# Polysketch attention with a phase mixer: wide numerator products, matrix-half sums on VectorE, a balance by ScalarE and a new order behind the first part

## The chip, the cores and the metric

One core of one Trainium2 chip runs the whole program. TensorE multiplies matrices into PSUM (eight banks of 512 32-bit words in each of 128 partitions), VectorE, ScalarE and GpSimd compute elementwise, and SyncE (SP), ScalarE and GpSimd issue DMAs. The metric is the device time of one execution in microseconds (us); lower is better. Where this text says "the profile", it means one execution taken by the hardware profiler, with a page of tables and a trace of single instructions behind it.

## The reference

The shapes are B = 4 batches, H = 4 heads, S = 1088 positions, D = 32 numbers a head, r = 8. An attention with the product features phi(x) = (S1 x) outer (S2 x), 64 numbers, gives x of 1088 x 128 for each batch; a phase mixer follows:

```python
def phi(x):
    a = np.einsum('rd,bhsd->bhsr', S1, x)
    b = np.einsum('rd,bhsd->bhsr', S2, x)
    return np.einsum('bhsi,bhsj->bhsij', a, b).reshape(*x.shape[:-1], r * r)
q_p, k_p = (phi(q), phi(k))
kv = np.einsum('bhsf,bhsd->bhfd', k_p, v)
z = np.sum(k_p, axis=2)
num = np.einsum('bhsf,bhfd->bhsd', q_p, kv)
den = np.einsum('bhsf,bhf->bhs', q_p, z)[..., None] + 1e-06
x = (num / den)                        # then (B,H,S,D) -> (B,S,H*D)
theta = x @ w_theta
zr, zi = x * np.cos(theta), x * np.sin(theta)
y = np.einsum('ts,bsd->btd', w_tok_r, zr) + np.einsum('ts,bsd->btd', w_tok_i, zi)
u = x + y
out = u + np.maximum(u @ w_ch, 0.0)
```

The weights (S1, S2, and the four of the mixer) come as 64-bit floating-point words.

## The kernel before

**How it is written.** No loop of the program runs on the chip in the order of its source. Each piece of work is an `Op` (an engine, a function that emits a few instructions, the buffers that it writes and reads), numbered as it is created by `Layout.op` (L203). A table of numbers, `ORDER` (L34), says in which order all 1020 operations are emitted, and each engine then runs its own ones strictly in that order. An operation that must wait holds up everything behind it on the same engine. A second table, `STARTS` (L80), gives each operation a planned start. `run` (L248) uses it to give buffers their places: memory is divided into classes of equal slots (L344: "big" 22 of 1152 words a partition, "zs" 5 of 2176, "hf" 6 of 576, "g3" 5 of 768, "g1" 6 of 384, "sm" 13 of 192, "ps" the eight PSUM banks and so on). `issue` (L267) uses it to put small matmuls without use (`spin`, L427, into a bank that nobody reads) into planned gaps of TensorE during the first part, from operation `first` (39 spins) to operation `last`.

**Stages.** (1) The 64-bit weights are unpacked into 32-bit ones on the chip: for each of 17 rows of the token matrix w_tok (128 x 1088, loaded by SP), two ScalarE passes (L643, L645) and two VectorE steps. (2) From k and v come the sums `kv` and the row sums for the denominators, batch by batch (batches 2 and 3 together). (3) From q come the levels, products of q with the sketch in several exact slices (`levels`, L1034; its function `whole`, L1049, multiplies by a stationary block of 128 positions at a time, nine blocks, though the last one has 64 real positions only). (4) `outputs_x` (L1088) makes x. (5) theta, the cosines and sines and z = (x cos, x sin) follow. (6) The token mix multiplies z by the rows. Batches 0 and 1 do it directly (`mix_row`, L1256; 17 rows, three column pieces). Batches 2 and 3 are done together by `winograd` (L1352): seven half-size products in place of eight. (7) `finish` (L1282) multiplies by w_ch, adds, transposes and stores.

**outputs_x for batches 2 and 3** (`QUADS`). The nine chunks of 128 positions are worked in three groups of three. For each group VectorE forms the outer products `qp` (768 numbers a partition, L1101), transposes them in blocks of 32 x 32 into `qt` (L1109), and the operation `quads` (L1112) multiplies: 32 matrix products, each with a stationary 32 x 32 tile of the sums `bd` and 96 moving columns (3 chunks x 32 positions), into four PSUM banks `xq`. Four ScalarE copies (L1121) then bring the banks into `xT`. The three groups are three such rounds a batch, six in both; a product of 32-bit numbers leaves two matmul records in the trace.

**balance** (L1229). The two batches' x are scaled to like size before they are mixed: VectorE reduces each `xT` (1152 numbers a partition) to the maximum of magnitudes (L1232), five short steps keep only the exponents of the two maxima (`ratio`, L1235) and form powers of two. ScalarE scales x of batch 3 by one of them (`even`, column 4), and VectorE takes it out again at the end (`add`, column 5). Any number of about the right size would serve, since only its exponent is used and what is multiplied is divided again.

**turn** (`XTURN`, batches 1 to 3). x is needed in the other orientation too. VectorE transposes in 32 x 32 blocks (L1160), SP writes the result to DRAM (`far`, L1161) and reads it back in four DMAs in another arrangement (L1165).

**winograd** (L1352). The four quarters of the token matrix (rows by imaginary or real part and column half of 544) are combined by `asum` ("1" to "4", eight differences or sums of 128 x 544 each), z by `zsub`. The products "1", "2", "5", "6", "3", "7", "4" run in this order of creation, each in two column parts of 384 and 160 (`PARTS`), eight matmuls a part. `APOOL` (L153) names the sums that GpSimd makes:

```python
APOOL = ("4", "3")
...
E, e = (G, "G") if name in APOOL else (V, "V")          # in asum
```

After a product, `add` (VectorE) brings its bank into `xT`; `ends` multiplies the 64 last positions; `done` calls `finish` for each part.

**finish and the end.** `finish` multiplies by w_ch, adds max(u w_ch, 0) to u (VectorE), and `turn` (L1302) transposes and, for the first half of batch 3 (`ends`), issues the four stores in the same operation: one by ScalarE, one by SP, two by GpSimd. The last 160 columns of this half go through `finish_turned` (L1329) instead: two TensorE transpositions, a ScalarE copy into the free part of `xT` (L1338), two products, all in one operation, then a VectorE step and two stores.

Of the kernel before, what the change touches and what calls it, by code (L numbers as in the profile page):

```python
# [10 lines left out]
F32 = mybir.dt.float32  # L11
# [67 lines left out]
)  # L79
STARTS = (  # L80
# [58 lines left out]
)  # L139
WARM = 0  # L140
FILL = 5.0
LOAD_LEAD = 60.0
RAW_LEAD = 30.0
CHAINS = ((0,), (1,), (2, 3))
# [1399 lines left out]
```

## Time and profile before

| What | Value |
|---|---|
| runs | 217.95, 218.06, 217.34 us; median 217.95 |
| profiled execution, first start to last end (span) | 215.9 us |
| TensorE busy (PE) | 208.9 us, 97% of the span |
| TensorE weight loads (PEld) | 152.8 us, 71% |
| VectorE busy (DVE) | 174.3 us, 81% |
| ScalarE busy (ACT) | 114.5 us, 53% |
| GpSimd busy (POOL) | 59.7 us, 28% |
| sums of matrix halves on GpSimd, 128 x 544 | 16 of 1458 ns, 22.1 us |
| sums and differences on VectorE, 128 x 544 | 8 of 1204 ns (`asum` "2") and 8 of 715 ns (`asum` "1") |
| numerator products, 32x32 tiles with 96 columns | 384 records, 5.8 us busy in sum, mean 252 ns |
| their ScalarE copies, L1121 | 24 of 252 ns |
| largest magnitudes by VectorE, L1232 | 2 of 1344 ns |
| ScalarE pass that also sums, L991 | 1170 ns, and 199 ns to read the sum |

In the profile's rows, "L399" is the line of the kernel that emits the instruction; many have the line of a helper (L399 is `mm`, L379 `tt`, L386 `stt`). "ps<-big,zs" names the class of the output and of the inputs. "128*128" is the tile of TensorE that a matmul uses (rows x columns), then follow shape and type of the moving operand, and "x10" is the number of records. Records of TensorE are pipelined and overlap, so a mean duration is not the time that one takes from the engine; the distance of the starts is. A bracket such as "[2.70 <-PE ps L399]" says how long the engine stood idle ahead of the instruction, in us, and what ended that.

### The profile page before, as it was taken

To read this page: it belongs to the slowest core of one execution; us is meant where nothing else is said; L and a number is where in the kernel's file an instruction comes from. 1 tells how busy PE (TensorE), PEld (TensorE's weight loads), DVE (VectorE), ACT (ScalarE), POOL (GpSimd) and SP (SyncE) were. 2 spreads that over 40 slices of the span, in tenths; PEclk is the share of its full clock that TensorE was granted. 3 is DMA by queue.
4 is the path that set the end of the run, shared out by engine and by line. 5 is a ranking of instruction groups with operands and counts; after the bars stand their busy time and mean duration, and the time that the engine had idled before them with its cause. 6 is when DMAs were issued, how large, how long until landed. Compare 5 with 4: busy or idle time off the path is not lost.

```text
span 215.9 us, 5832 instructions
## 1 busy us (share of the span) xinstructions
PE 208.9 (97%) x2396; PEld 152.8 (71%) x2396; DVE 174.3 (81%) x343; ACT 114.5 (53%) x256; POOL 59.7 (28%) x105
## 2 busy tenths in 40 slices
PE   7899999999999999999999999999999999999992
PEld 7677798868866666866668666667677776666781
DVE  1799998999999998999999798885994747456263
ACT  4899989999998895798704233363810000000000
POOL 1272740306400000604004100000006489950403
PEclk9999999999999999999999999999999999999998
DMA  6999999995998993192002402424050420010735
GB/s 222 395 418 419 384 365 420 425 315 97 360 285 267 416 432 145 75 308 45 0 0 32 74 3 112 114 109 112 2 88 15 67 39 0 0 23 8 125 55 103
DMA packets 28046, 37.09 MB, mean 172 GB/s; under 512 B 20564, under 2 KB 23044, under 8 KB 25844
## 3 DMA queue, kind: packets, MB, share of 16 engines
q1 hardware_dynamic: 22868, 31.86, 42.4%
q0 software_dynamic: 1552, 3.25, 7.2%
q10 hardware_dynamic: 3600, 1.62, 2.8%
q8 instruction: 19, 0.31, 0.6%
q14 instruction: 7, 0.06, 0.1%
HBM read 29.84 MB, written 4.00 MB: 157 GB/s over the span
## 4 chain that ended last, share of the span: by engine, by line
PE 63%; DMA 18%; ACT 14%; issue 2%; SPq 1%; DVE 1%; POOL 1%; POOLq 0%; ACTq 0%
PE ps L399 61%; DMA zs<-w_tok 13%; DMA big<-k_l 5%; ACT big L645 4%; ACT big L643 3%; ACT lv L1056 1%; PE ps L1131 1%; ACT big L1021 1%; ACT g L1199 1%; ACT g L1202 1%; ACT g L1205 1%; ACT g L1203 1%; POOL out L1299 1%; SPq L671 0%; ACT g L1135 0%
## 5 line engine op out<-in xcount | busy, mean ns | idle before, releaser
L399 PE MATMUL ps<-big,zs 128*128 128x384 f32 (+2 forms) x380 | 110.5, 436 | 0.0
L399 PEld LDWEIGHTS ps<-big,zs 128*128 128x128 f32 x380 | 66.9, 190 | 32.5
L379 POOL TENSOR_TENSOR big<-big,big 128x544 f32<-128x544 f32 x16 | 22.1, 1458 | 48.6 <-DVE big L379 44.6
L399 PE MATMUL ps<-big,big 128*32 128x32 f32 (+2 forms) x352 | 22.8, 234 | 0.0
L643 ACT ACTIVATE big<-zs 128x1088 f32<-128x1088 f32 x17 | 20.9, 1231 | 1.5 <-DMA zs<-w_tok 0.9
L379 DVE CUSTOM_DVE_ANT_0 big<-big,big 128x2176 uint16<-128x2176 uint16 x17 | 21.5, 1275 | 0.0
L645 ACT ACTIVATE big<-zs 128x1088 int32<-128x1088 uint32 (+1 forms) x18 | 21.4, 1194 | 0.3 <-DMA zs<-w_tok 0.3
L1338 ACT COPY big<-ps 80x256 f32<-80x256 f32 x1 | 0.4, 368 | 39.6 <-DMA out<-g 39.6
L399 PEld LDWEIGHTS ps<-big,big 128*32 128x32 f32 (+1 forms) x352 | 15.3, 124 | 6.8 <-issue 0.8
L1276 ACT COPY g<-ps 128x384 f32<-128x384 f32 (+1 forms) x6 | 2.5, 466 | 23.4 <-PE ps L399 23.4
L379 DVE TENSOR_TENSOR big<-big 128x544 f32<-128x544 f32 x8 | 9.5, 1204 | 5.6 <-PE ps L399 5.6
L383 DVE TENSOR_SCALAR big<-big 128x1088 int32<-128x1088 int32 x17 | 12.2, 719 | 0.0
L379 POOL TENSOR_TENSOR mf<-mv,sm 128x32 f32<-128x32 f16 (+1 forms) x3 | 0.8, 262 | 39.1 <-DVE sm L379 39.1
L428 PE MATMUL ps<-idle 128*128 128x112 bf16 (+1 forms) x67 | 10.0, 312 | 1.3 <-POOL idle L430 1.3
L379 DVE TENSOR_TENSOR g<-lv 128x768 f32<-128x768 f32 x12 | 11.1, 950 | 0.1
L399 PEld LDWEIGHTS ps<-w,big 128*128 128x128 f32 (+1 forms) x76 | 9.8, 189 | 1.4
L379 DVE TENSOR_TENSOR big<-big,hf 128x1152 f32<-128x1152 f32 x8 | 10.7, 1351 | 0.0
L399 PE MATMUL ps<-w,big 128*128 128x128 f32 (+1 forms) x76 | 10.5, 278 | 0.0
L399 PE MATMUL ps<-sbk,g 128*128 128x64 f32 x72 | 10.0, 276 | 0.3 <-ACT g L793 0.3
L379 DVE TENSOR_TENSOR zs<-zs,g 128x384 f32<-128x384 f32 (+2 forms) x24 | 9.8, 447 | 0.2
L386 DVE SCALAR_TENSOR_TENSOR big<-ps,even,big 128x384 f32<-128x384 f32 (+1 forms) x10 | 4.8, 493 | 6.3 <-PE ps L399 6.2
L1199 ACT ACTIVATE g<-ps 128x384 f32<-128x384 f32 x12 | 5.9, 504 | 7.3 <-PE ps L399 7.3
(199 smaller groups left out, 379.2 us busy)
## 6 DMA issues: line engine op xcount, KB each, us to landing
zs<-w_tok SPq DMA_DIRECT2D x17, 1088.0 KB, 10.6
big<-k_l SPq DMA_DIRECT2D x5, 576.0 KB, 13.2
big<-v_l SPq DMA_DIRECT2D x4, 576.0 KB, 15.6
big<-q_l SPq DMA_DIRECT2D x3, 576.0 KB, 10.7
big<-hf POOLq DMA_DIRECT2D x3, 576.0 KB, 10.0
far<-zs SPq DMA_DIRECT2D x3, 576.0 KB, 2.8
zs<-far SPq DMA_DIRECT2D x12, 144.0 KB, 4.3
big<-k_l ACTq DMA_DIRECT2D x2, 576.0 KB, 4.4
```

The costliest lines, as they stand in the source:

```text
L379: eng.tensor_tensor(out=o, in0=a, in1=b, op=f)
L383: (eng or V).tensor_scalar(out=o, in0=a, scalar1=s1, scalar2=s2, op0=op0, **kw)
L386: (eng or V).scalar_tensor_tensor(out=o, in0=a, scalar=s, in1=b, op0=op0, op1=op1)
L399: T.matmul(o, lhs, rhs, start=start, stop=stop, skip_group_check=True)
L428: T.matmul(nowhere()[:, :n], idle()[:, 0:P], idle()[:, :n], start=True, stop=True, skip_group_check=True)
L643: op("A", 0.22 + n * 0.0009, lambda: A.activation(dfn(), words_of(raw(), n)[1].bitcast(F32), AF.Prelu, scale=2.0**-112, alpha=-(2.0**32)), ...
L645: op("A", 0.22 + n * 0.0009, lambda: A.activation(stp(), words_of(raw(), n)[0].bitcast(U32), AF.Copy, scale=2.0**-29), [stp], [raw])
L1021: op("A", act(GW) + 0.1, lambda g=g, tr=tr: A.activation(f()[:, g * GW:(g + 1) * GW], tr(), AF.Copy, scale=s()[:, 0:1]), [(f, g)], [tr, (s ...
L1056: op("A", act(480), lambda g=g, lp=lp: A.copy(lv().rearrange("p l (c n) -> p l c n", n=HR)[:, :, g * GC:(g + 1) * GC], lp().rearrange("p c ...
L1131: T.transpose(tr()[:, i * P:(i + 1) * P], qp()[:, i * H + 2 * n:i * H + 2 * n + 2].rearrange("p h i j -> p (h i j)"), ident())
L1199: op("A", act(GW), lambda cs=cs, th=th: A.activation(cs()[:, 0], th(), AF.Copy, bias=ROUND), [(cs, 0)], [th])
L1276: op("A", act(w), lambda: A.copy(u(), yp()[:, :w]), [uT], [yp])
```

## The change

1. **Numerator.** For batches 2 and 3, `qt` is one buffer of class "zs" for all nine chunks (2304 words, so the class grows from 2176). The three groups' outer products and transpositions are made as before; then one `quads` makes 32 products of 288 columns into four banks, followed by four copies of 288 columns.
2. **Sums of halves.** `APOOL` is empty: `asum` "3" and "4" go to VectorE like "1" and "2".
3. **Balance.** In place of VectorE's maximum, ScalarE passes over `xT` with the function Abs and an accumulator; the passes' output goes to a scratch buffer "dump" of class "hf". `ratio` is unchanged.
4. **finish_turned** is split into four operations (transpositions, ScalarE copy, products, VectorE step) and the two stores, and its result has a buffer `yb` of class "g1" of its own.
5. **whole** in `levels` uses, for the last chunk, a stationary block of the 64 real positions only.
6. **Order.** The first 265 operations of `ORDER` stay as they are but for operations 0 and 1 (the memset of `idle` and the 39 spins), which are now named first. All that follows is in another order. `STARTS` is gone: `GAPS` says after which operations of the first part a `spin` is emitted (27 in all, and the one at `last`, as before), and `SLOTS` gives each of 393 buffers its slot.
7. **Classes.** "hf" goes from 6 slots to 5 and "sm" from 13 to 12.

At the end of the new order TensorE has product 3's first part (384 columns) up to its last matmul, then the output product of batch 2's second half (its second part), the transpositions and the products of the turned piece, and last the output product of batch 3's first part, `out3_0_0`. VectorE ends with the two sums from PSUM, batch 2's last step and transposition, the turned piece's step, and then the step of `out3_0_0` and its `turn` with the four stores. In the order before, `out3_0_0` stood ahead of product 3's second part.

```diff
 ORDER = (
-    29, 32, 4, 2, 5, 0, 1, 3, 34, ...
+    0, 1, 29, 32, 4, 2, 5, 3, 34, ...
...
-STARTS = (
+GAPS = {11: 3, 57: 3, 79: 3, 110: 1, 203: 8, 153: 1, 77: 5, 86: 2, 163: 1}
+SLOTS = (
...
-APOOL = ("4", "3")
+APOOL = ()
...
     def run(self):
-        slots = {c: [[0.0, None] for _ in range(n)] for c, (n, _) in self.classes.items()}
...
         self.order = [self.ops[i] for i in ORDER]
-        for o, at in zip(self.order, STARTS):
...
+        for b, slot in zip([b for b in self.bufs if b.cls is not None], SLOTS):
+            b.slot = slot
...
         for o in self.order:
-            if o.eng == "P":
...
+            for _ in range(GAPS.get(o.i, 0)):
+                fill()
...
-        "zs": (5, 2176),
+        "zs": (5, 2304),
...
-        "hf": (6, 576),
+        "hf": (5, 576),
...
-        "sm": (13, 192),
+        "sm": (12, 192),
...
             def whole(g=g, o=o):
                 for i in range(GC):
-                    x = f()[:, (g * GC + i) * P:(g * GC + i + 1) * P]
-                    mm(o(i)[:, 2 * HR:], x, mf[b]().rearrange("p t h r -> p (t h r)"), False, i == GC - 1)
+                    c = g * GC + i
+                    n = min(P, S - c * P)
+                    x = f()[:, c * P:c * P + n]
+                    mm(o(i)[:n, 2 * HR:], x, mf[b]().rearrange("p t h r -> p (t h r)"), False, i == GC - 1)
...
+        qt = buf("zs", (NC, H, 2, SQ), F32, "qt") if b in QUADS else None
...
             if b in QUADS:
-                qt = buf("g3", (GC, H, 2, SQ), F32, "qt")
-                xq = [buf("ps", (GC, SQ), F32, "xq") for _ in range(NQ)]
...
+                vop(CH * R * R, lambda g=g, qp=qp: V.transpose(
+                    out=qt()[:, g * GC:(g + 1) * GC].rearrange("p c h f t -> p (c h f t)"),
+                    in_=qp().rearrange("p n i j -> p (n i j)")), [(qt, g)], [qp])
                 continue
...
+        if b in QUADS:
+            xq = [buf("ps", (NC, SQ), F32, "xq") for _ in range(NQ)]
+
+            def quads():
+                for f in range(2):
+                    for j in range(NQ):
+                        for h in range(H):
+                            u = slice(j * SQ, (j + 1) * SQ)
+                            mm(xq[j]()[h * D:(h + 1) * D], bd()[u, f, h], qt()[u, :, h, f], f == 0, f == 1)
+
+            op("P", QUAD, quads, xq, [bd, qt], hold=[xt])
+            for j in range(NQ):
+                op("A", act(NC * SQ), lambda j=j: A.copy(
+                    xt().rearrange("p (c j t) -> p c j t", j=NQ, t=SQ)[:, :, j], xq[j]()), ...)
...
-            vop(NC * P, lambda j=j, b=b: V.tensor_reduce(out=even()[:, j:j + 1], in_=xT[b](), axis=AX.X, op=ALU.max,
-                                                         apply_absolute_value=True), [(even, j)], [xT[b]])
+            dump = buf("hf", (NC * P,), BF16, "dump")
+            op("A", act(NC * P) + 0.1, lambda j=j, b=b, dump=dump: A.activation(
+                dump(), xT[b](), AF.Abs, accum_out=even()[:, j:j + 1]), [dump, (even, j)], [xT[b]])
...
     def finish_turned(b, t0, w, u, keys, due):
-        y = lambda: xT[b]()[:n, 0:2 * DM]
+        yb = buf("g1", (2 * DM,), F32, "yb")
+        y = lambda: yb()[:n]
...
+        op("P", 0.2, turned, [pu], keys, hold=[yb])
+        op("A", act(2 * DM), lambda: A.copy(y(), pu()[:n, 0:2 * DM]), [yb], [pu])
+        op("P", 0.35, products, [po], keys + [w2])
+        vop(2 * DM, lambda: stt(y(), po()[:n, 0:2 * DM], 0.0, y(), ALU.max, ALU.add), [yb], [po])
```

More of the change, by code (lines that the diff above doesn't have):

```diff
@@ L44 @@
     163, 164, 165, 166, 211, 39, 191, 167, 173, 448, 114, 168, 212, 175, 244, 449, 331, 176, 192, 177, 266, 450, 336,
[34 rows of a table removed]
-)
-STARTS = (
[58 rows of a table removed]
[33 rows of a table added]
+)
+GAPS = {11: 3, 57: 3, 79: 3, 110: 1, 203: 8, 153: 1, 77: 5, 86: 2, 163: 1}
+SLOTS = (
[11 rows of a table added]
 )
 WARM = 0
-FILL = 5.0
 LOAD_LEAD = 60.0
@@ L157 @@
 UDMA = (True, True, False, False)
-TILE16, TILE32, TILE64, QUAD = 0.045, 0.12, 0.15, 0.65
+TILE16, TILE32, TILE64, QUAD = 0.045, 0.12, 0.15, 1.25
 ADD_FLY = 9.0
@@ L248, in run, with issue @@
     def run(self):
-        slots = {c: [[0.0, None] for _ in range(n)] for c, (n, _) in self.classes.items()}
-        for b in self.bufs:
-            b.left = len(b.ops)
         self.order = [self.ops[i] for i in ORDER]
-        for o, at in zip(self.order, STARTS):
-            o.start = at / 100.0
-            o.end = o.start + o.dur + o.fly
-            for b in o.bufs:
-                if b.slot is None and b.cls is not None:
-                    free = [(s[0], i) for i, s in enumerate(slots[b.cls]) if s[1] is None]
-                    b.slot = min(free)[1]
-                    slots[b.cls][b.slot][1] = b
-            for b in o.bufs:
-                b.left -= 1
-                b.end = max(b.end, o.end)
-                if not b.left and b.slot is not None:
-                    slots[b.cls][b.slot] = [b.end, None]
-    def issue(self, pools, fill, span):
-        last, on = 0.0, False
-        for o in self.order:
-            if o.eng == "P":
-                if on:
-                    for _ in range(int((o.start - last - 0.08) * FILL)):
-                        fill()
-                last, on = o.end, on and o is not span[1] or o is span[0]
+        for b, slot in zip([b for b in self.bufs if b.cls is not None], SLOTS):
+            b.slot = slot
+    def issue(self, pools, fill):
+        for o in self.order:
+            for _ in range(GAPS.get(o.i, 0)):
+                fill()
             for b in o.bufs:
@@ L430 @@
     op("G", 0.3, lambda: G.memset(idle(), 0.0), [idle], [], due=-20.0)
-    first = op("P", 3.2, lambda: [spin(112) for _ in range(39)], [nowhere], [idle], due=-10.0)
+    op("P", 3.2, lambda: [spin(112) for _ in range(39)], [nowhere], [idle], due=-10.0)
     op("V", 1.25, constants, [hm, bdm, halfpi, ones], [])
@@ L1145, in outputs_x @@
                cells(xt, g * GW, (g + 1) * GW), [xp])
+        if b in QUADS:
+            at("num", b)
+            xq = [buf("ps", (NC, SQ), F32, "xq") for _ in range(NQ)]
[8 more added lines that the diff above has]
+                op("A", act(NC * SQ), lambda j=j: A.copy(
+                    xt().rearrange("p (c j t) -> p c j t", j=NQ, t=SQ)[:, :, j], xq[j]()), [(xt, ("q", j)) if j < NQ - 1 else xt], [xq[j]])
         src = xt
@@ L1331, in finish_turned, with turned @@
         n = w // 2
-        y = lambda: xT[b]()[:n, 0:2 * DM]
-        def products():
-            parts = [u()[:, c * n:(c + 1) * n] for c in range(2)]
-            for c, uc in enumerate(parts):
-                T.transpose(pu()[:n, c * DM:(c + 1) * DM], uc, ident())
-            A.copy(y(), pu()[:n, 0:2 * DM])
-            for c, uc in enumerate(parts):
-                mm(po()[:n, c * DM:(c + 1) * DM], uc, w2()[:, 1], True, True)
-        op("P", w * 4 / 2400 + 0.01, products, [po, pu], keys + [w2])
-        vop(w, lambda: stt(y(), po()[:n, 0:2 * DM], 0.0, y(), ALU.max, ALU.add), keys, [po])
-        vop(w, lambda: None, [], keys)
+        yb = buf("g1", (2 * DM,), F32, "yb")
+        y = lambda: yb()[:n]
+        def turned():
+            for c in range(2):
+                T.transpose(pu()[:n, c * DM:(c + 1) * DM], u()[:, c * n:(c + 1) * n], ident())
+        def products():
+            for c in range(2):
+                mm(po()[:n, c * DM:(c + 1) * DM], u()[:, c * n:(c + 1) * n], w2()[:, 1], True, True)
+        op("P", 0.2, turned, [pu], keys, hold=[yb])
+        op("A", act(2 * DM), lambda: A.copy(y(), pu()[:n, 0:2 * DM]), [yb], [pu])
+        op("P", 0.35, products, [po], keys + [w2])
+        vop(2 * DM, lambda: stt(y(), po()[:n, 0:2 * DM], 0.0, y(), ALU.max, ALU.add), [yb], [po])
         def store(E, c):
             E.dma_start(out[b, t0 + c * n:t0 + (c + 1) * n, :], y()[:, c * DM:(c + 1) * DM])
-        op("S", w * P * 2 / 100e3, lambda: store(SY, 0), [], keys, due, lk=2)
-        op("A", 0.92, lambda: store(A, 1), [], keys, due, fly=2.1)
+        op("S", w * P * 2 / 100e3, lambda: store(SY, 0), [], [yb], due, lk=2)
+        op("A", 0.92, lambda: store(A, 1), [], [yb], due, fly=2.1)
     def winograd(t):
@@ L1469 @@
         if not bs[0]:
-            last = op("P", 0.1, spin, [nowhere], [kvb[WARM]] if WARM < B else [idle])
+            op("P", 0.1, spin, [nowhere], [kvb[WARM]] if WARM < B else [idle])
     for b in range(B):
@@ L1499 @@
     with tc.manual_schedule():
-        L.issue(pools, spin, (first, last))
+        L.issue(pools, spin)
 def kernel(q, k, v, S1, S2, moe_w_theta, moe_w_tok_r, moe_w_tok_i, moe_w_ch):
```

13 lines of the change are left out of this document (removed), and 138 rows, old and new, of tables (ORDER, SLOTS, STARTS).

## The prediction

> **What bounds the kernel now.** I read the page first, then the TensorE rows by shape for 140 to 210 us, then the timeline of single engines.
>
> ```profile
> span 215.9 us, 5832 instructions
> PE 208.9 (97%) x2396; PEld 152.8 (71%) x2396; DVE 174.3 (81%) x343; ACT 114.5 (53%) x256; POOL 59.7 (28%) x105
> ...
> PE 63%; DMA 18%; ACT 14%; issue 2%; SPq 1%; DVE 1%; POOL 1%; POOLq 0%; ACTq 0%
> ```
>
> Busy PE is modelled, so 97% proves little by itself. Counting does: from 140 to 210 us the rows by shape hold 154 records of 384 columns, 120 of 160, 12 of 320 and 12 of 128. Starts in the timeline stand 0.325, 0.135, 0.27 and 0.11 us apart (136.99 to 137.64 for two of 384, 207.59 to 207.86, 149.92 to 150.46, 138.93 to 139.59 for six). 154 x 0.325 + 120 x 0.135 + 12 x 0.27 + 12 x 0.11 = 70.8 us in 70: TensorE is full. The same count comes out near the length of the window back to about 45 us, and the list of TensorE's waits after 45 us holds one of 0.2 us. So from 45 us on the time is TensorE's work, any wait that the new order opens, and what follows its last large product.
>
> ```profile
> 67.38 0.48 PE L399 MATMUL ps<-big,big 128*32 128x32 f32 x32
> ...
> 77.49 0.88 PE L399 MATMUL ps<-g,big 128*32 128x64 f32 x48
> ...
> 119.09 0.96 PE L399 MATMUL ps<-g,g 32*32 32x96 f32 x64
> 119.98 3.39 PE L399 MATMUL ps<-big,zs 128*128 128x384 f32 x10
> ```
>
> Second number: from first start to last end; the start of the next row tells what a block takes. One numerator block (32 products, 64 records: a 32-bit product leaves two) holds TensorE for 119.98 - 119.09 = 0.89 us, 13.9 ns a record. The rows after the first two start at 67.79 and 78.42: 12.8 ns a record at 32 columns, 19.4 at 64.
>
> ```profile
> 208.50 2.34 PE L399 MATMUL ps<-big,zs 128*128 128x160 f32 x16
> ...
> 210.30 0.57 DVE L1303 STREAM_TRANSPOSE g<-big 128x384 f32<-128x384 f32 x1
> ...
> 210.68 0.43 PE L399 MATMUL ps<-big,w 128*128 128x160 f32 x2
> 210.88 0.38 DVE L386 SCALAR_TENSOR_TENSOR big<-ps,even,big 128x160 f32<-128x160 f32 x1
> 211.17 1.81 POOL L1299 DMA_DIRECT2D out<-g  x3 [0.50 <-DVE g L1303]
> ```
>
> The end: the last large product hands over at T = 210.68; GpSimd's three store issues run from 211.17 to 212.98, so the last starts at 212.38 = T + 1.7 (the last of SP and ScalarE start at 212.79 and 212.73, T + 2.1); the span ends at T + 5.2.
>
> **Numerator products.** Six blocks of 96 columns become two of 288: the same 64 records each, three times as wide. No row shows 32x32 tiles at 288. Lower bound: width is free, 0.89 us a block. Upper: time goes with columns, 2.67. Nearest rows: with four tiles side by side, 32 more columns cost 19.4 - 12.8 = 6.6 ns, 0.206 ns a column; with sixteen tiles a quarter of that, 0.052. So 13.9 + 192 x 0.052 = 23.8 ns a record, 1.5 us a block; I take that. Sum: 6 x 0.89 = 5.34 becomes 3.0, **-2.3 us** (-3.6 to 0). The copies on ScalarE fall from 24 of 252 ns to 8 of about 0.41 us (384 columns take 0.49); from 120 to 160 us ScalarE is 24 to 62% busy, so that is worth nothing to the end. The block now waits for all three transposed groups and four free banks, and the rows of batch 1 stand behind it on TensorE, with their PSUM readers on ScalarE behind those. Before, the third group was ready at 134.4 for a block at 135.35, 0.9 us ahead; in the new order the last bank and the last group come about as far ahead, so 0 (at most 1 us for each of the two blocks if that cover is gone).
>
> **The end.** In the new order the last large record is the 384-wide one of product 3, then TensorE has out2_1_1, the two transpositions, the two products of the turned piece, and last the 384-wide output product out3_0_0, which before came at 207.86, ahead of 16 large records. So T comes 0.65 us earlier (one pair of 384). After T, by rows: VectorE takes the sum from PSUM to T + 0.8 (0.2 handover, 0.61), out2_1_1's two steps to 1.4, the turned piece to 1.8 (its copy on ScalarE is done by 1.05); TensorE needs 0.27 + 0.2 + 0.43 before out3_0_0 starts at 0.9, which ends at 1.55; VectorE's two steps of it run from 1.85 to 2.9. Only then are its four stores issued (they sit inside the transposing step `turn`), two of them by GpSimd at 0.62 us each: the last issue starts at T + 3.75 against T + 1.7. **+2.05 - 0.65 = +1.4 us** (0.2 to 2.05: if the stores of SP and ScalarE land last in both, it is T + 2.95 against T + 2.1, +0.85 - 0.65; at the other end T comes no earlier).
>
> **Sums of halves on VectorE.**
>
> ```profile
> 175.66 5.47 POOL L379 TENSOR_TENSOR big<-big,big 128x544 f32<-128x544 f32 x4
> ...
> 177.13 4.59 DVE L379 TENSOR_TENSOR big<-big 128x544 f32<-128x544 f32 x1 [2.70 <-PE ps L399]
> ```
>
> Sixteen sums leave GpSimd (1.458 us each, 22.1 busy) and join VectorE at 0.64 (two in 1.36 less the overlap): +10.3 us. VectorE idles some 26 us after 140, so they fit; had they no cover, each late one would cost 0.64 at the product that reads it. One difference on VectorE took 4.59 us where its neighbours take 0.72, while GpSimd's sums ran; that 3.9 us goes. The Trainium skill, SBUF — State Buffer, "Who interferes with whom", says that a VectorE operation with two SBUF inputs and a GpSimd one exclude each other for a whole instruction. By that every GpSimd sum would hold VectorE, up to 22 us; the trace shows one such hold, and other pairs of the two that overlapped unharmed (162.84 to 164.2), so the row decides: 3.9 us of a spare engine.
> I checked in the new order where these results are read. The tightest: product 7's third row needs its sum and the sum from PSUM of product 6; those come 2 to 4 us ahead. Product 4's first matmul follows the last of product 7 by 0.8 us, and needs the 0.6 us read of that bank plus 0.2: **+0.1 us**.
>
> **Balance on ScalarE.** Two VectorE reductions (1.344 us each) become two ScalarE passes with an accumulator; the row of the same form (line 991) is 1.17 plus 0.2. Path of batch 3 from the end of its numerator block: 0.2 + 4 copies 1.65 + 1.37 + the ratio 0.85 + two theta copies that ScalarE does first, 0.15 beyond the ratio + scaling 1.25 + transposition 1.4 + trip through DRAM 6.4 (142.26 to the end of its transfers at 148.7) + z and first difference 2.0 = 15.3 us. TensorE has queued between (counted: 6 + 6 large of 0.645, 12 of 0.272, seven rows of batch 1, three theta, one output product) 17.7 us. Cover 2.4 us, so 0.
>
> **Moves.** The first 265 operations keep their order on every engine; the spin and its memset, now written first, were first on their engines before. Fills stay 28. After that all queues are in another order; SP's changes most: the load of v2 goes behind batch 1's trip through DRAM and row 12. From the last numerator product of batch 1 TensorE has 15.7 us of work (counted in the new order) before the first product with v2. In that time: copy 0.7, transposition 1.4, first half of the trip 2.9, its four read issues 1.75, v2's issue 0.4, together 7.2 us; loads of this size land 4.4 us (k on ScalarE's queue) to 15.6 us (v on SP's, amid others) after issue, so v2 is 4.1 us early to 7.1 late. Between the ends: row 16 and the same trip, 2.3 MB like the new row 12, trip and v2, were moved between 90 and 98.5 us, which puts v2 some 5 us after its issue, 3.5 early. I take 0. The last chunk's `whole` product loads 64 columns where it loaded 128: 8 loads less by half of 0.11, at most -0.4; **-0.1**, since the stream then limits. The turned piece in a tile of its own, smaller pools and fixed slots add no instruction but one split; each first use of a bank that I followed is freed before, save the 0.1 above.
>
> **Sum:** -2.3 + 1.4 + 0.1 - 0.1 = -0.9 on 215.9 gives a span of 215.0. The median of the runs is 217.95, 2.05 above the span; so **217.0 us**.
>
> **Rivals.** (1) Slower: the wide blocks are bound by their columns. For it: 32 to 64 columns already costs half as much again. Against: four-tile records of 64 columns run far under their lone time of over 50 ns. It decides from where two blocks save less than the end costs, (5.34 - 1.4)/2 = 1.97 us a block; at 2.67 the sum is 0 + 1.4 = +1.4, 219.4. (2) A new wait in the reordered middle: the v2 load or batch 3's trip under traffic. For: both now stand near their use, DMA is at full rate until 80 us. Against: the covers above. At 1 us it eats the gain (217.0 + 1.0 = 218.0, no change); at 3 us 220.0. (3) Width is almost free, 0.97 a block, and the late stores land beside each other: -3.4 + 0.2 - 0.1 = -3.3, 214.7; half-way to the forecast 215.8. (4) The saving is not taken by the path at all, since records hide TensorE's idle time: for it the modelled ends, against it the count of 70.8 in 70; 219.4 like (1), and counted there.
>
> **Chances.** Forecast 0.44 (own range 216.2 to 217.8), (3) 0.17, (2) 0.26, of which 0.12 without change, (1) with (4) 0.13. A move of 0.3%, 0.65 us, is about what a measurement of this kernel can tell. Of the forecast 0.08 lies within that. Faster 0.36 + 0.17 = 0.53, same 0.08 + 0.12 = 0.20, slower 0.14 + 0.13 = 0.27. The range reaches from between (3) and its half-way point to the price of (1) and a wait of 2.6 us in (2): 215.3 to 219.6.
>
> **What would show it.** Records of 32x32 with 288 columns: 128, next row 1.5 us after a block's start; 0.9 or 2.7 refute my price. The last four stores 2.9 us after the last large product, end of span at T + 7.3. No GpSimd sum and no difference over 1 us on VectorE. A TensorE wait above 0.5 us between 60 and 205 us, on v2, on z of batch 3 or on a sum, proves me wrong in (2).

## The result and the profile after

The changed kernel is slower: 226.5 us median (224.46 to 227.36), before 217.82 in the same runs, ratio 1.0379 (1.0346 to 1.0412). The profiled execution has a span of 225.4 us against 215.9. It is one of the two longest of the four executions, whose spans are 222.6 to 225.4 us at mean granted clocks of 0.977 to 0.967.

The page of the changed kernel; the row of slices that begins with PE is that of TensorE, the one that begins with PEclk its granted clock in tenths:

```profile
span 225.4 us, 5309 instructions
PE 215.0 (95%) x2140; PEld 154.4 (68%) x2140; DVE 179.0 (79%) x357; ACT 116.2 (52%) x244; POOL 38.6 (17%) x89
...
PE   7899999995999999999999999999999999999990
...
PEclk9999999997559999999999999999999999999999
```

Two things are new: a slice at about 53 us in which TensorE is half idle, and three slices, this one and the two behind it, in which its clock is not 1.0. The timeline of TensorE (start, length, engine, instruction; in brackets the idle time ahead and what ended it), then that of GpSimd with one row of SP, all of the changed kernel:

```profile
51.44 0.20 PE L332 MATMUL ps<-hf 128*32 128x32 bf16 x4
53.95 1.60 PE L332 MATMUL ps<-mf,big 128*128 128x96 f32 x6 [2.32 <-POOL mf L316]
...
72.06 2.10 PE L332 MATMUL ps<-big,zs 128*128 128x384 f32 x6
```

```profile
36.52 0.42 SPq L647 DMA_DIRECT2D big<-k_l  x1
...
41.11 0.73 POOL L519 COPY mf<-mf 128x64 f32<-128x64 f32 x1
51.25 1.09 POOL L326 DMA_DIRECT2D big<-hf  x1 [9.41 <-DMA big<-k_l]
52.36 1.15 POOL L312 TENSOR_TENSOR mf<-mv,sm 128x32 f32<-128x32 f16 x1
53.60 0.30 POOL L316 TENSOR_SCALAR mf<-mf 128x32 f32<-128x32 f32 x1
```

GpSimd stands for 9.4 us at an accumulating DMA (`keys2`, the keys of batch 2, through `join`), whose input is a load of k that SP issued at 36.52 and that landed at 50.7. Behind it in the same queue are the two steps that finish `mf` of batch 1, and TensorE waits 2.3 us for those. In the kernel before, the two stood ahead of that DMA:

```profile
49.98 0.24 POOL L379 TENSOR_TENSOR mf<-mv,sm 128x32 f32<-128x32 f16 x1 [9.16 <-DVE sm L379]
50.31 1.45 POOL L383 TENSOR_SCALAR mf<-mf 128x32 f32<-128x32 f32 x1
...
54.21 0.90 POOL L393 DMA_DIRECT2D big<-hf  x1
```

Table by stage of the changed kernel (stretch, its length, busy time of the five engines with instruction counts, granted clock, DMA share, GB/s):

```profile
53.00:53.50 0.50, 0.00 (x0) 0.00 (x0) 0.50 (x2) 0.00 (x0) 0.50 (x1) 1.00 1.24 302
53.50:54.00 0.50, 0.04 (x1) 0.05 (x1) 0.38 (x1) 0.00 (x0) 0.41 (x3) 0.59 1.10 286
54.00:54.50 0.50, 0.50 (x3) 0.50 (x3) 0.00 (x0) 0.00 (x0) 0.40 (x3) 0.50 1.29 295
...
67.00:67.50 0.50, 0.50 (x10) 0.05 (x10) 0.50 (x2) 0.00 (x0) 0.00 (x0) 0.76 0.00 0
```

Some 2 us after TensorE fell idle (at 51.63) its clock is halved, just as the work comes, and stays so from 53.6 to 67.2 us, though TensorE is busy from 53.95 on. The wait costs far more than its own length. The stretch isn't equally long in every execution: the mean clock of 0.977 in the one of 222.6 us leaves room for 10.2 us at half clock, against the 13.65 of the profile.

What I had priced is there too: the two wide numerator blocks, and the end.

```profile
137.09 1.60 PE L332 MATMUL ps<-zs,g 32*32 32x288 f32 x64
138.62 1.99 PE L332 MATMUL ps<-big,zs 128*128 128x320 f32 x6
...
217.92 0.43 PE L332 MATMUL ps<-big,w 128*128 128x160 f32 x2
218.19 0.38 PE L1275 MATMUL ps<-ident,big 128*80 128x128 f32 x2
...
218.84 0.86 PE L332 MATMUL ps<-big,w 128*128 128x384 f32 x2
```

A block takes 138.62 - 137.09 = 1.53 us. The end comes 7.5 us after 217.92 (the start of out2_1_1's product, T of the prediction).

### The profile page after: what moved, and what is told of

Read it like the earlier page. It is cut to its first block, busy times and chain, and to the rows that moved or that the text cites. A ratio compares the mean times of both kernels' runs of the same rounds, so it can differ in the third digit from the quotient of the medians.

```text
span 225.4 us, 5309 instructions
## 1 busy us (share of the span) xinstructions
PE 215.0 (95%) x2140; PEld 154.4 (68%) x2140; DVE 179.0 (79%) x357; ACT 116.2 (52%) x244; POOL 38.6 (17%) x89
## 4 chain that ended last, share of the span: by engine, by line
PE 74%; DMA 19%; POOL 1%; DVE 1%; ACT 1%; issue 1%; SPq 1%; POOLq 0%; ACTq 0%
PE ps L332 72%; DMA big<-k_l 11%; DMA zs<-w_tok 7%; PE ps L1053 1%; ACT lv L991 1%; PE ps L1126 1%; POOL mf L312 1%; POOL big L326 0%; SPq L604 0%; DVE lv L312 0%; POOL out L1237 0%; ACT big L576 0%; POOLq L1480 0%; DVE g L1241 0%; DVE big L319 0%
## 5 line engine op out<-in xcount | busy, mean ns | idle before, releaser
L332 PE MATMUL ps<-big,big 128*32 128x32 f32 (+2 forms) x352 | 22.0, 242 | 0.0
L312 DVE TENSOR_TENSOR big<-big,big 128x544 f32<-128x544 f32 x24 | 16.7, 716 | 0.4 <-PE ps L332 0.2
L326 POOL DMA_DIRECT2D g<-big x6 | 5.3, 978 | 59.0 <-ACT g L1214 48.7
L332 PE MATMUL ps<-mf,big 128*128 128x96 f32 (+1 forms) x72 | 12.7, 319 | 2.3 <-POOL mf L316 2.3
L1237 POOL DMA_DIRECT2D out<-g x8 | 5.0, 631 | 49.0 <-DVE g L1241 49.0
L332 PEld LDWEIGHTS ps<-mf,big 128*128 128x128 f32 (+1 forms) x72 | 10.6, 217 | 3.2 <-POOL mf L316 2.4
L991 ACT COPY lv<-ps 128x480 f32<-128x480 f32 x12 | 6.6, 556 | 10.6 <-PE ps L332 10.6
L332 PE MATMUL ps<-w,big 128*128 128x128 f32 (+1 forms) x76 | 11.6, 294 | 0.0
L332 PEld LDWEIGHTS <-hf 128*32 128x32 bf16 (+1 forms) x252 | 8.0, 101 | 3.4 <-issue 2.2
## 6 DMA issues: line engine op xcount, KB each, us to landing
big<-v_l SPq DMA_DIRECT2D x4, 576.0 KB, 13.2
```

What stands on the lines that cost most here:

```text
L312: eng.tensor_tensor(out=o, in0=a, in1=b, op=f)
L326: op("G", 0.9, lambda: G.dma_start(dst(), src(), accum_op=ALU.add), w, r, fly=fly)
L332: T.matmul(o, lhs, rhs, start=start, stop=stop, skip_group_check=True)
L991: op("A", act(480), lambda g=g, lp=lp: A.copy(lv().rearrange("p l (c n) -> p l c n", n=HR)[:, :, g * GC:(g + 1) * GC], lp().rearrange("p c ...
L1237: E.dma_start(out[b, s0:s0 + n, f * SQ:(f + 1) * SQ].rearrange("(c j) i -> j c i", j=SQ), ot()[f * SQ:(f + 1) * SQ, :n].rearrange("j (c i) ...
```

## The experiments

Twelve kernels ran, each beside the kernel before on the same chip; a ratio is to that kernel, its interval behind it. Versions are compared with one another by these ratios. Where ORDER is changed, the diff shows the order of the operations that moved, by their names.

### The queue's head: join_behind

```diff
 GpSimd's order
-    ..., blocks_m(3), keys2 (accumulating DMA), chain1 (mf of batch 1), kvb1, ...
+    ..., blocks_m(3), chain1 (mf of batch 1), keys2 (accumulating DMA), kvb1, ...
```

> The changed kernel with one pair of GpSimd operations exchanged: the accumulating DMA of batch 2's keys (it waits for a load that lands at 50.7 us) goes behind the two GpSimd steps of batch 1's mf instead of ahead of them. Theory A (the queue's head blocks, and TensorE's wait of 2.3 us costs the half clock from 53.5 to 67.2 us): no TensorE wait at mf, granted clock 1.00 there; 2.3 + 13.6 x 0.5 = 9.1 us less, 226.5 - 9.1 = 217.4. Rival B (the clock drops for another reason, from the work around it): only the 2.3 us go, 224. Rival C (the rest of the new order is what costs): 222 or more, with waits elsewhere.

219.92 us, ratio 1.0073 (1.0049 to 1.0097); span 217.7 against 225.4. GpSimd and TensorE of join_behind:

```profile
48.87 0.25 POOL L314 TENSOR_TENSOR mf<-mv,sm 128x32 f32<-128x32 f16 x1 [6.24 <-DVE sm L314]
49.20 0.30 POOL L318 TENSOR_SCALAR mf<-mf 128x32 f32<-128x32 f32 x1
50.52 0.90 POOL L328 DMA_DIRECT2D big<-hf  x1 [1.01 <-DMA big<-k_l]
```

```profile
51.54 0.20 PE L334 MATMUL ps<-hf 128*32 128x32 bf16 x4
51.67 0.91 PE L334 MATMUL ps<-mf,big 128*128 128x96 f32 x6
...
64.43 2.10 PE L334 MATMUL ps<-big,zs 128*128 128x384 f32 x6
```

The wait is gone, the granted clock is 1.00 from 50 to 70 us, and the DMA itself loses nothing by standing second, since its load lands after both steps. That is theory A. Its size was 1.4 us too big: from the mf product to the product of the third row of the token mix (64.43) TensorE takes 12.76 us; in the changed kernel the same stretch, 53.95 to 72.06, took 18.11. So the half clock cost 5.4 us in its 13.6, not 6.8; not all that TensorE does there goes by its clock (six large records take 3.78 us from start to start in place of 2.03, a piece of twelve small ones 0.20 in place of 0.18). 2.3 + 5.4 = 7.7 us of the span. By the ratios, over all executions, it is 3.1% or 6.7 us, less than in the profiled execution. Rival B is out; of rival C 1.6 us are left, taken up below.

### Is it idleness that halves the clock: spins_in_gap

```diff
             for _ in range(GAPS.get(o.i, 0)):
                 fill()
+            if o.i == 540:
+                keep = view(pools["ps"](0), (384,), F32)
+                for _ in range(14):
+                    fill(384, keep)
```

(Operation 540 is the product that waits for mf; bank 0 is free there.)

> The changed kernel as it is, and 14 matmuls without use (384 columns, some 0.16 us each, 2.24 us) ahead of the product that waits for mf. The wait for the DMA stays, but TensorE isn't idle in it. Theory A: the granted clock stays 1.00, only the 2.3 us remain: 226.5 - 6.8 = 219.7. Rival B (the half clock isn't due to idle TensorE): clock 0.5 again, 226.5.

223.69 us, ratio 1.0231 (1.0200 to 1.0261). Table by stage of spins_in_gap:

```profile
50.00:60.00 10.00, 10.00 (x191) 7.86 (x190) 5.95 (x8) 6.21 (x12) 4.46 (x11) 1.00 0.88 228
60.00:70.00 10.00, 8.21 (x208) 5.41 (x207) 9.20 (x20) 9.35 (x19) 0.00 (x0) 1.00 0.69 259
```

The clock stays 1.00 with the DMA still blocking (mf is ready at 53.6 here too): it is the idleness of TensorE that halves it. The time was 4 us over the expectation. 1.8 us of that is a second stand that only this kernel has:

```profile
66.00 0.27 PE L338 MATMUL ps<-big,big 128*32 128x32 f32 x8
68.06 2.10 PE L338 MATMUL ps<-big,zs 128*128 128x384 f32 x6 [1.79 <-issue]
```

The profile names no releaser. One packet of the instruction queue (16 KB) is on its way from 65.75 to 66.70, so TensorE may have run out of instructions; that wasn't tried. Another 1.4 is that the expectation gave the half clock 6.8 us where it cost 5.4. By spans the two account for it: 225.4 - 5.4 + 1.8 = 221.8, measured 222.0; most of the 0.8 us that are left of the 4 is the distance between the median of the changed kernel (226.5) and its profiled execution (227.13).

### The same blockage in the kernel before: before_join_ahead

```diff
 GpSimd's order, kernel before
-    ..., chain1 (mf of batch 1), blocks_m(2), kvb1, keys2, ...
+    ..., keys2, chain1 (mf of batch 1), blocks_m(2), kvb1, ...
```

> The kernel before, with only the accumulating DMA of batch 2's keys moved ahead of batch 1's mf steps on GpSimd. There TensorE asks for mf at 53.4 us, 1.6 us after it is ready; the move makes it ready some 2 us later. Theory A: a TensorE wait of 0.3 to 1.2 us at that product, too short for the clock to fall: 218.1 to 219.0. Rival (any wait there throws the clock to half for 13 us): 225 or so. If the load lands earlier than in the changed kernel: no wait, 217.8.

219.4 us, ratio 1.0029 (0.9999 to 1.0058). GpSimd of before_join_ahead, and its TensorE:

```profile
51.76 0.57 POOL L383 TENSOR_TENSOR mf<-mv,sm 128x32 f32<-128x32 f16 x1
52.43 0.84 POOL L387 TENSOR_SCALAR mf<-mf 128x32 f32<-128x32 f32 x1
```

```profile
53.77 1.48 PE L403 MATMUL ps<-mf,big 128*128 128x96 f32 x12
```

The same exchange makes mf 1.5 us late (ready at 53.3, before at 51.8) and TensorE doesn't notice: here it comes to that product at 53.8. The blockage costs only where TensorE's new order asks 2.1 us sooner, at 51.64. Both moves are needed. The span is 1.8 us above before all the same; 1.3 of it is a TensorE wait for ScalarE, up to 80.1 us, that the profile of before doesn't have.

### The end: join_old_tail and join_tail2

```diff
 join_old_tail, TensorE's and VectorE's last operations
+    m3_0 (last four), m3_1 (two), out2_1_0, m4_1 (two), out3_0_0, m4_1 (three), m3_1 (last), out2_1_1, turned piece
+    acc3_0, step and transposition of out2_1_0, step of out3_0_0, acc4_1, then the transpositions of out3_0_0, out3_1_0, out3_1_1, then acc3_1
 join_tail2
+    m3_0 (three), out2_1_0, m3_0 (last), m3_1, m4_1 (three), out3_0_0, m4_1 (two), m3_1 (last three), out2_1_1, turned piece
+    transpositions of out3_1_0 and out3_1_1, acc4_0, ..., step of out3_0_0, acc4_1, transposition of out3_0_0, acc3_1, ...
```

> As join_behind, and the end in the order of before: product 3's last four large products of 384 columns ahead, and out3_0_0 with its step, transposition and stores ahead of product 4's last rows. My prediction's end term says 1.4 us less than join_behind (216.0). Rival: the stores of SP and ScalarE end last either way, 0.2 us less (217.2).

> join_behind with another order of the last 12 us on all engines: the two transpositions and the stores of batch 3's second half as soon as they can be, product 3's first part and out3_0_0 with its step and stores some 2 us ahead of the last large product, which is product 3's last of 160 columns. The turned piece ends it, as before. By my end term: 1.4 to 2 us less than join_behind. Rival (SP's and ScalarE's last stores end it either way): 0.5 us less or nothing.

The first missed: 221.2 us, ratio 1.0128 (1.0086 to 1.0169). I had put three transpositions on VectorE ahead of the last sum from PSUM, which the turned piece waits for, and seven stores behind one another on SP. VectorE and TensorE of join_old_tail:

```profile
211.48 1.26 DVE L1243 STREAM_TRANSPOSE g<-big 128x384 f32<-128x384 f32 x3
212.66 0.34 DVE L321 SCALAR_TENSOR_TENSOR big<-ps,even,big 128x160 f32<-128x160 f32 x1
```

```profile
213.06 0.41 PE L1277 MATMUL ps<-ident,big 128*80 128x128 f32 x2 [0.90 <-DVE big L321]
```

The second: 218.05 us, ratio 1.0009 (0.9988 to 1.0029), so 0.64% or 1.4 us below join_behind. From the start of TensorE's last record to the end of the span it takes 4.0 us, like the kernel before, where join_behind takes 6.1. The order of the end is worth what the prediction said.

### The numerator: join_quads96

```diff
                 def quads():
+                    for g in range(NG):
+                        c = slice(g * GC, (g + 1) * GC)
                     ...
-                    mm(xq[j]()[h * D:(h + 1) * D], bd()[u, f, h], qt()[u, :, h, f], f == 0, f == 1)
+                    mm(xq[j]()[h * D:(h + 1) * D, c], bd()[u, f, h], qt()[u, c, h, f], f == 0, f == 1)
```

> join_behind with the numerator of batches 2 and 3 in the same place as one operation, but in three passes of 96 columns (192 records) in place of one of 288 (64). If width is what saves: 2 x (2.67 - 1.53) = 2.3 us more than join_behind. Rival (what is saved is taken up by a wait behind it): less than 1 us more.

221.17 us, ratio 1.0136 (1.0113 to 1.0159): 0.63%, 1.4 us above join_behind. The 192 records of a batch take 2.35 us (the starts of all 384 stand 4.69 us apart in sum, those of the 128 wide ones 3.06); the six separate blocks of before had 5.35. So width saves 1.6 us, of which 1.4 show in the time, and another 0.7 comes from fewer blocks: together the 2.3 of the prediction. The expectation had 2.3 for the width alone, since it took a pass of 96 columns inside one operation to cost as much as a block of its own.

### TensorE's tile: join_merged and join_whole128

join_behind still lies 1.8 us of span above before. By the starts in the trace TensorE's records other than the numerator's stand 2.0 us further apart in sum than before, without one large wait. Two rows of join_behind that hold the same six records, and what follows each:

```profile
57.51 2.10 PE L334 MATMUL ps<-big,zs 128*128 128x384 f32 x6
59.54 0.20 PE L334 MATMUL ps<-hf 128*32 128x32 bf16 x4
...
59.83 2.10 PE L334 MATMUL ps<-big,zs 128*128 128x384 f32 x6
61.76 0.27 PE L908 MATMUL ps<-ident,sm 128*128 128x128 f32 x1
```

59.54 - 57.51 = 2.03 us where a tile of 128 x 32 follows, 61.76 - 59.83 = 1.93 where the tile stays 128 x 128. A last record takes 93 ns more ahead of another tile, at other widths too (416 against 323 ns at 384 columns, 363 against 269 at 320, 205 against 112 at 96, in join_behind as in before), and small tiles ahead of a large one lose as much or more. After 45 us the trace of before changes tile 23 times apart from the numerator, that of join_behind 46 times; 23 changes at 93 ns would be 2.1 us, an estimate.

```diff
 join_merged, TensorE's order between 50 and 62 us
-    levels 1 (exact), sums2, levels 1 (exact), sums3, levels 1 (whole), sums3 x3, theta, sums3 x4, levels 1, ...
+    levels 1 (all), theta, then sums3, sums2 and rest3 in one piece
 join_whole128
-                    n = min(P, S - c * P)
-                    x = f()[:, c * P:c * P + n]
-                    mm(o(i)[:n, 2 * HR:], x, ...)
+                    mm(o(i)[:, 2 * HR:], f()[:, c * P:(c + 1) * P], ...)
```

> join_behind with TensorE's order changed between 50 and 62 us alone: the products on 128x32 tiles of batches 2 and 3 (sums2, sums3, rest3), which stand in small pieces between the levels products of batch 1 on 128x128 tiles, are put together behind them. Theory D (each change of the tile's shape costs TensorE some 0.1 us; the trace of join_behind has 94 changes, that of before 76; a product ahead of one starts its successor 93 ns later than within its group): about 12 changes fewer, 1.2 us less than join_behind. Rival (the distances are a matter of the record, other work fills them): same as join_behind, within 0.3 us.

> join_behind with the last chunk of whole back at a stationary block of 128 positions (the last block's upper rows of the result are computed and not used, as before the change). By theory D the narrower block is a tile of its own shape: two changes for each of four batches, some 0.15 to 0.25 us a batch: 0.6 to 1.0 us less than join_behind. My prediction had it the other way: 0.1 to 0.4 us more.

join_merged: 220.46 us, ratio 1.0119 (1.0077 to 1.0162), which is not less than join_behind; whether it is more, the intervals don't tell. Between 50 and 62 us TensorE's distances do shrink, by 0.9 us in sum, with 13 changes fewer. Then comes what the profile of join_merged shows, and that of join_behind doesn't:

```profile
91.30 2.02 PE L334 MATMUL ps<-big,zs 128*128 128x384 f32 x6
94.49 0.91 PE L334 MATMUL ps<-big,zs 128*128 128x384 f32 x2 [1.17 <-DVE zs L314]
```

TensorE waits 1.2 us for z of batch 1, which VectorE makes from x that comes back from DRAM (in join_merged at 93.88). In join_behind the same product follows the one ahead of it with no gap, and VectorE has that x at 92.63. It is not that TensorE came too soon for an unchanged trip: the four reads back were issued earlier than in join_behind (from 85.43 against 86.07) and took longer (6.3 us against 4.7 in the median). Up to there join_merged is 0.6 us ahead (the mf product at 90.66 against 91.25), behind the wait 0.8 us late, and so it stays to the end. So the changes of tile are shown in place, but what they are worth to the end is not, and why the reads took longer in this execution is open. join_whole128: 219.46 us, ratio 1.0065 (1.0042 to 1.0088), span 217.5: by the intervals no difference to join_behind. The mf products stand 0.8 us closer, but 0.5 us of it is given back at one place, at 62 us.

### Sums and balance: tail2_pool_sums and tail2_dve_balance

```diff
 both from join_tail2
-APOOL = ()
+APOOL = ("4", "3")                                   # tail2_pool_sums
-            op("A", ..., A.activation(dump(), xT[b](), AF.Abs, accum_out=even()[:, j:j + 1]), ...)
+            vop(NC * P, ... V.tensor_reduce(out=even()[:, j:j + 1], in_=xT[b](), ..., op=ALU.max), ...)   # tail2_dve_balance
```

> join_tail2 with the sums 3 and 4 back on GpSimd. My prediction had the move to VectorE as worth nothing: same as join_tail2 within 0.4 us, with VectorE operations that stand still beside GpSimd's (some us in sum). Rival (the sums on GpSimd come too late for products 7 and 3, or hold VectorE): 1 us and more above join_tail2.

> join_tail2 with the largest magnitudes by VectorE again (two reductions of 1.34 us) in place of ScalarE's sums. My prediction had the move as worth nothing: same as join_tail2 within 0.4 us. Rival (VectorE is the fuller one there and the reductions push z of batches 2 and 3 back): a TensorE wait at z and 0.5 us or more above join_tail2.

With GpSimd's sums: 220.81 us, ratio 1.0131 (1.0112 to 1.0150), 1.2% or 2.6 us above join_tail2. TensorE, GpSimd and VectorE of tail2_pool_sums, then the same VectorE operation in join_tail2:

```profile
193.64 3.83 PE L334 MATMUL ps<-big,zs 128*128 128x384 f32 x18 [1.51 <-POOL big L314]
```

```profile
167.44 1.33 POOL L314 TENSOR_TENSOR big<-big,big 128x544 f32<-128x544 f32 x1 [1.33 <-DVE big L314]
167.50 1.69 DVE L314 TENSOR_TENSOR zs<-zs 128x384 f32<-128x384 f32 x1
```

```profile
168.37 0.55 DVE L314 TENSOR_TENSOR zs<-zs 128x384 f32<-128x384 f32 x1
```

A sum takes GpSimd 1.34 us there and VectorE 0.72; the new order has the products at the places where VectorE's sums are ready. Besides, GpSimd's sums hold VectorE, as the expectation had it: five of its operations, which start while a sum runs and read two inputs from SBUF, take 7.5 us there and 2.1 in join_tail2. TensorE's new waits are 1.51 us for GpSimd and 0.50 and 0.34 for VectorE, 2.35 of the 2.6 us. In this order the move is a condition, not a nothing. With VectorE's maxima: 218.62 us, ratio 1.0032 (1.0007 to 1.0058), against 1.0009 (0.9988 to 1.0029): the intervals overlap, at most some 0.5 us. Its profile has a TensorE wait of 0.53 us for VectorE at batch 3's numerator block (142.09), which join_tail2's doesn't have.

### The numerator alone in the old order: before_wide and before_wide_late

```diff
 kernel before, outputs_x
+                if g < NG - 1:                       # of the three groups only the last one has work
+                    op("P", 0.0, lambda: None, [], [])
...
+                op("P", 1.5, quads, xq, [bd, qt], hold=[xt])      # 32 products of 288 columns
 before_wide_late, TensorE's order
-    num3, mix1_1, out0_1, mix1_1, mix1_1, theta3_0, theta3_1, ...
+    mix1_1, out0_1, mix1_1, mix1_1, num3, mix1_0, mix1_2, mix1_0, mix1_1, theta3_0, theta3_1, ...
```

> The kernel before with the numerator's part of the change alone: two operations of 288 columns in place of six of 96, where the last group of each batch stood, theta of the group concerned two to three products later; pools as in the change. All else as before, also GpSimd's sums, the balance by VectorE and the end. By my term, which join_quads96 bore out: 2.3 us less than before, 215.7. Rival (the order of before has covers for 96 columns only, the later x makes a wait): 217 or more, with a wait at theta or z.

> before_wide with batch 3's wide numerator block four products of 384 columns (2.6 us) later on TensorE, and theta of its groups four products behind it. In before_wide TensorE asked for the third transposed group at 131.35 us, VectorE delivered at 134.0, TensorE stood for 2.8 us and ran at half clock until 137.5. If that wait is all that took the gain: no wait over 0.5 us after 60 us, granted clock 1.00, and the whole 2.3 us show: 215.7. Rival (VectorE or the trip of batch 3 through DRAM then makes a wait further on): 217 or more.

before_wide: 219.81 us, ratio 1.0052 (1.0015 to 1.0090). The rival held. VectorE, then TensorE, then the table by stage, all of before_wide:

```profile
133.01 0.98 DVE L1114 STREAM_TRANSPOSE zs<-g 128x768 f32<-128x768 f32 x1
```

```profile
130.00 1.35 PE L403 MATMUL ps<-big,zs 128*128 128x384 f32 x4
134.14 2.58 PE L403 MATMUL ps<-zs,g 32*32 32x288 f32 x64 [2.78 <-DVE zs L1114]
```

```profile
134.00:137.00 3.00, 2.86 (x65) 1.44 (x66) 2.96 (x4) 0.45 (x2) 0.00 (x0) 0.51 0.33 108
137.00:138.00 1.00, 1.00 (x3) 0.54 (x3) 0.00 (x0) 1.00 (x4) 0.00 (x0) 0.77 0.58 150
```

VectorE delivers the third group of batch 3 at 134.0, hardly sooner than before (134.5); TensorE, which has two blocks less to do by then, is there at 131.35, waits 2.8 us and then works at half clock for 3.4: the saving turned into a wait and the wait into a slower clock. Not in every execution: three of the twelve kept a mean clock of 0.997 or more and took 217.45, 218.15 and 218.62 us, the others had 0.984 to 0.992 and took 219.06 to 220.89. So this order loses the clock often, not always; only one execution has a trace. With four products moved ahead of the block (before_wide_late) it is 216.3 us, ratio 0.9923 (0.9893 to 0.9952), 1.8 us under the kernel before. That is the best of all versions here, faster than both kernels. Its profiled execution is the longest, 219.3 us, so its time isn't read here. It does show the wait at the block gone:

```profile
136.75 1.75 PE L403 MATMUL ps<-zs,g 32*32 32x288 f32 x64 [0.20 <-DVE zs L1114]
```

Further on, at 147.80, TensorE waits 0.96 us for VectorE there, as the rival had it. Whether that is the half microsecond that lacks to 2.3 was not tested.

## Why the prediction was wrong, point by point

**The step that failed** is the one under "Moves": "After that all queues are in another order; SP's changes most". I followed SP's queue to v2, and TensorE's inputs in the late stages, and concluded a cover; GpSimd's queue between 39 and 56 us I did not go through. There a DMA with a wait of its own was put ahead of two short steps that TensorE wants, and TensorE's order asks for them 1.7 us sooner (51.64 against 53.37). Both orders can be read from the diff, and that the load lands at about 50 was to be had from the kernel before (SP issues it at 36.59; loads of k take 13.2 us there in the median). Its TensorE:

```profile
53.37 1.48 PE L399 MATMUL ps<-mf,big 128*128 128x96 f32 x12
```

**The price of a wait** failed too. Rival (2) had the mechanism, "a new wait in the reordered middle", and priced it at its own length, 1 us for 1 us. The profiles show 2.3 us of wait and 5.4 us of half clock. The trace of before held a row for it, at its end, after the last matmul (same columns as above):

```profile
212.00:213.00 1.00, 0.17 (x2) 0.00 (x0) 0.42 (x1) 0.14 (x1) 0.98 (x2) 1.00 0.75 128
213.00:214.00 1.00, 0.00 (x0) 0.00 (x0) 0.00 (x0) 0.00 (x0) 0.00 (x0) 0.89 0.82 177
214.00:215.00 1.00, 0.00 (x0) 0.00 (x0) 0.00 (x0) 0.00 (x0) 0.00 (x0) 0.50 0.07 18
```

The clock falls to half 1.6 us after TensorE's last work (212.17). That is one case and no threshold: at the ends of the other traces the fall comes 1.5 to 5.1 us after the last work. From 45 us on the kernel before has no wait over 0.2 us, so a first one of over 2 us should have had a rival of its own, with a slow stretch behind it.

**The sum against the runs.** Of the 9.5 us of span, 7.7 are this wait with its clock (join_behind). The rest is +1.8, where I had -0.9. By the distances in the traces of join_behind and before it adds up: the numerator -2.3, TensorE's other records +2.0, and +2.1 from the start of its last record to the end (6.1 against 4.0). By terms:

| Term | predicted | measured, by what |
|---|---|---|
| numerator | -2.3 (1.5 us a block) | -2.3 (1.53 us a block; join_quads96) |
| end | +1.4 | +1.4 (join_tail2); last store issue T + 3.9, predicted T + 3.75 |
| sums on VectorE | 0 | 24 sums and differences of 716 ns, none held; 2.6 us if undone in the new order (tail2_pool_sums) |
| balance on ScalarE | 0 | 0 to 0.5 saved (tail2_dve_balance) |
| narrow last block of `whole` | -0.1 | 0.8 us more in its own products, nothing that can be told in the time (join_whole128) |
| order of TensorE's small products | not seen | 23 more changes of tile, 93 ns and more each; 2.0 us of distances in all |
| v2 | 0 | no TensorE wait on it; the tight one is batch 1's trip |

Numerator and end were right in mechanism and size, and the wait that the prediction named as the sign of being wrong ("a TensorE wait above 0.5 us between 60 and 205 us, on v2, on z of batch 3 or on a sum") came at 51.6 us on none of these. That tile changes cost was in my own rows: I had read 19.4 against 12.8 ns a record from blocks of one kind, and never compared a block's last record by what follows it. Of the 2.0 us only 0.9 were shown to go with the changes (join_merged); how the rest is divided stays open.

One reading of the trace was too kind, though it changed no term. I took the pair of a VectorE and a GpSimd operation at 162.84 to 164.2 us for unharmed. VectorE had started first there, and it was GpSimd's sum that took longer, 1.75 us where 1.34 is usual; in tail2_pool_sums, where GpSimd starts first, VectorE stands.

## What to carry to other kernels

When an order is rewritten, go through every in-order queue and ask, of each instruction that waits for something far (a DMA's landing above all), what short work stands behind it and when the bounding engine wants that: exchanging two operations here was worth 6.7 to 7.7 us and cost nothing. Price a new wait of a bounding TensorE together with the clock that it can lose. And a saving on one engine counts only up to the next engine's delivery: before moving work forward, look how far ahead its other inputs are, and fill the room with work that is ready, as before_wide_late does.

## What the runs showed of the hardware that was not expected

- After short waits TensorE was granted half its clock: in the changed kernel 2.0 us after it fell idle (at 53.6 us), in before_wide 2.7 us after (at 134.1). Fourteen matmuls without use in the gap kept it at 1.00 (spins_in_gap). It took 13.65 us of nearly full work to come back in the first case and 3.41 us in the second; why they differ is open. The Trainium skill, TensorE: Matmul & The Clock Gate, Part 1: The HAM clock gate, has the half clock after an idle window of about 3.4 us and the full one after one busy window of that length: here a shorter idle time was enough, and the return took up to four times as long.
- The length of a wait alone did not decide it. Waits of 1.79 us (spins_in_gap, up to 68.06) and 1.34 us (before_join_ahead, up to 80.10) left the clock at 1.00; one of 1.33 us (before_wide_late, up to 79.62) was followed by half clock from 80.18 to 83.59. In all fourteen traces the stretches between two changes of the clock are whole multiples of 3.41 us (47.79, 13.65 and 157.01 us in the changed kernel, 129.71, 3.41 and 78.51 in before_wide). So it may matter where in these steps a wait falls; that is argued from the traces, no run moved a wait against them.
- Where a GpSimd sum and a VectorE operation with two inputs from SBUF overlap, the one that started later was slowed. In tail2_pool_sums, VectorE operations that started second took 1.33 to 1.69 us (the same take 0.29 to 0.55 in join_tail2); where VectorE was first, GpSimd's sums took 1.38 to 1.58 us in place of 1.34. A VectorE operation with one input from PSUM, amid a sum at 187.22, took 0.52 us, no more than elsewhere.
- A change of TensorE's tile costs the last record ahead of it 93 ns (2.03 against 1.93 us for the same six records).
- 32x32 products at 288 columns with 32-bit numbers: 23.9 ns a record (1.53 us / 64), against 12.2 at 96 columns in one operation (2.35 / 192) and 13.9 in blocks of their own.
